# Eight places for the last Q, K, V rows, their summed stores on GpSimd's queue, and three small operations moved behind their neighbours

## The chip, the core and the metric

The kernel runs on one core of a Trainium2 chip. A core has a matrix engine (TensorE, PE in the rows), a vector engine (VectorE, DVE), a scalar engine (ScalarE, ACT), GpSimd (POOL) and a queue engine (SyncE, SP). Each engine works through its own list of instructions in order; engines wait for each other by semaphores. Three of them issue transfers (DMAs): SP, ACT and POOL, each by a queue of its own, and all transfers are served by the same 16 DMA engines. The metric is the device time of one launch in microseconds; lower is better.

## What is computed

The reference is one transformer block in float32 with attention and feed-forward side by side, for 2048 tokens of width 576:

```python
xn = _layernorm(x)                               # no learned scale
# attention: 32 heads of 18; token s sees s, s-2, ..., s-14
qkv = (xn @ wqkv).reshape(B, S, 3, H, Dh)
idx = pos[:, None] - 2 * arange(8)[None, :]
attn = softmax(where(idx >= 0, q . k[idx] * 18 ** -0.5, -1e9))
a = (attn @ v[idx]) @ wo
# feed-forward: 576 -> 4608 -> 576
h = xn @ w1 + b1
r = where(h > 0, h, 0)
out = x + a + (r * r) @ w2 + b2
```

## The kernel before

**Numbers in two parts.** The matrix engine takes a rounded float32 form. Each operand is kept as a rounded part ("hi", written by ACT as a copy) and the remainder ("lo", written by DVE as the operand minus hi). A product is three matmuls: hi x hi, hi x lo, lo x hi. So nearly every operand costs one ACT and one DVE instruction before PE may use it.

**Stages.** The tokens are four blocks of 512. The launch forms Q, K and V of blocks 0 and 1, runs their feed-forward pairs with block 0's second projection, then block 1's second projection; from about 547 us it forms Q, K and V of blocks 2 and 3 together (`phase_b0`, `quad_step`), then runs the feed-forward pairs of blocks 2 and 3 (`ffn_pair` with `s` = 1, pairs `p` = 0 to 17), and last block 3's second projection. The change lies where `quad_step` ends and the pairs begin, at about 612 to 685 us.

**`quad_step`.** The products of two token blocks with two weight groups are formed in seven products for eight (a Strassen scheme), in seven steps `s` for two chains `i`. Steps 4 to 7 each end one output row of 128 tokens by 432 numbers: ACT copies it from PSUM into a place of the tile `st` (line 1050); where a second term is to be added (steps 4 and 6), DVE adds it there (`tt`, line 108, form 128x432); then a DMA writes the place to the DRAM scratch `kvq` (line 1054). Rows without a sum are stored from ACT's queue, rows with a sum from SP's. `st` has four places, taken in turn (`rows_out % NJ`). A place is written again once the store before it has landed. 32 rows are stored; the last eight belong to the last of four half rounds, and its last two steps stand inside the first feed-forward pair as filler.

**`ffn_pair`.** For two token blocks and two 128-wide slices of the hidden layer it again forms seven products, T2, T3 and so on, in three PSUM banks `ba`, `bb`, `bc`. Two intermediates are copied out of `bb` by ACT: `u[:, 0]` (line 691, after T2) and `u[:, 1]` (line 723, after T3); PE may write the next product into `bb` only after that copy. DVE adds `bc` and `u[:, 1]` into `r1` (line 108, `r<-p,r`); PE may write the next product (B22) into `bc` only after that. Between the products stands the projection of the pair before (`work`, line 536, seven matmuls each).

**The small stacks.** From pair 2 on the 32 left-over input rows are packed into one extra matmul per product. Pair 1 prepares that: `stack_hi` (ACT, line 562) and `stack_lo` (DVE, forms 32x1024 and 32x512 `w1r<-w1r`) split the packed rows `LR["st"]`; `left_weight_hi` (ACT, line 595) and `left_weight_lo` (DVE, 64x896) split the weights. The unpacked rows come from DRAM by six loads `w1r<-xl` (line 552) on SP's queue, into a tile of the two-buffer pool `w1r`.

**Attention as side work.** `side(k)` does the next k steps of an attention generator on DVE: products `pr<-q,kv`, sums `lg<-pr`, then a maximum and a subtraction, then a step that begins with the exponential on ACT (line 396, `lg<-lg`) and goes on with a sum, a reciprocal and a product on DVE. `side(k, False)` stops ahead of the step with the exponential.

**What sets the order.** The program is written out by hand: each engine runs its instructions in the order in which the code emits them. DMAs raise counters that are taken in turn, eight for SP and ACT together and eight for POOL. A DMA that is to raise a counter first waits until the DMA eight places before it in the program, which raised the same counter, has landed.

Of the kernel before, what the change touches and what calls it, by code (L numbers as in the profile page):

```python
# [8 lines left out]
F32 = mybir.dt.float32  # L9
# [7 lines left out]
P = 128  # L17
# [4 lines left out]
NJ = TB // P  # L22
# [5 lines left out]
CG = HG * DH  # L28
QW = 3 * CG
# [10 lines left out]
T1, T3, B11, T2, B22, B21, LEFT, T4 = range(8)  # L40
# [5 lines left out]
def block_kernel(ctx: ExitStack, tc: tile.TileContext, x, xt, wqkv, wo, w1, b1, w2, b2, w1l, out):  # L46
    nc = tc.nc
    const = ctx.enter_context(tc.tile_pool(name="const", bufs=1))
    mt = ctx.enter_context(tc.tile_pool(name="mt", bufs=1))
    sb = ctx.enter_context(tc.tile_pool(name="sb", bufs=1))  # L50
# [56 lines left out]
    def tt(out, a, b, op):  # L107
        return nc.vector.tensor_tensor(out=out, in0=a, in1=b, op=op)  # L108
# [204 lines left out]
    qp, stage = {}, {}  # L313
# [107 lines left out]
    def side(k, exp=True):  # L421

        while k > 0:
            if current[0] is None:
                if not queue or queue[0][0] not in landed:
                    return k
                name, make = queue.pop(0)
                current[:] = [make(), None, name]
            if current[1] == "exp" and not exp:
                return k  # L430
            try:
                current[1] = next(current[0])
                k -= 1
            except StopIteration:
                current[0] = None
        return 0
# [38 lines left out]
    def w1_hi(n, k):  # L475
        w1s[n, k] = mt.tile([P, 2, 4, 2 * P], F32R, name="w1s", bufs=3)
        nc.scalar.activation(w1s[n, k][:, 0], raw1[n][:, 4 * k:4 * k + 4], AF.Copy)  # L477
# [33 lines left out]
    def w2_lo():  # L511
        i = los[0]
        los[0] += 1
        if i >= len(stream):
            return
        w = w2s[stream[i]]
        tt(w[:, DE:], raw2.pop(i)[:, :D], w[:, :D].bitcast(F32), ALU.subtract)
        load_w2(i + 3)
# [25 lines left out]
    ST, LW, LR = {}, {}, {}  # L544
# [16 lines left out]
    def stack_hi(to, v):  # L561
        nc.scalar.activation(to, v, AF.Copy)

    def stack_lo(to, v):
        rows = slice(L, 2 * L)
        tt(to[rows], v[rows], to[rows].bitcast(F32), ALU.subtract)
# [27 lines left out]
    def left_weight_hi(p):  # L594
        nc.scalar.activation(LW[p % 2], LR["w"], AF.Copy)

    def left_weight_lo(p):
        rows = slice(2 * L, P)
        tt(LW[p % 2][rows], LR["w"][rows], LW[p % 2][rows].bitcast(F32), ALU.subtract)
        load_left_weights(p + 1)  # L600
# [4 lines left out]
    def ffn_pair(s, p, work, first=False):  # L605
# [75 lines left out]
            stack_hi(LR["st"][:, 0:2], LR["a"][:, 0:2])  # L681
            stack_hi(ST[T4], LR["a"][:, 3])
        if not first:
            side(1 if p == 1 else 3 if s else 2 + p % 2, s == 1)
        work(0)
        product(bb, T2, ss(2))
        own_w2 = first and s == 1
# [10 lines left out]
        def splits():  # L698
            if not own_w2:
                w2_lo()  # L700
            if not last and not s:
                w1_hi(n + 1, 0)
            if ready:
                left_weight_hi(p + 1)
            if s and p == 1:
                stack_lo(LR["st"][:, 0:2], LR["a"][:, 0:2])
                stack_lo(ST[T4], LR["a"][:, 3])
                stack_hi(ST[T1], LR["s"][:, 0])
            if not own_w2:
                w2_hi()  # L710
            if not last and not s:
                w1_lo(n + 1, 0)
            if ready:
                left_weight_lo(p + 1)
            if not own_w2:
                w2_lo()

        if not first:
            splits()
# [3 lines left out]
        nc.scalar.activation(u[:, 1], bb, AF.Copy)  # L723
        r0, r1 = four(), four()
        tt(r1[:, 1], bc, u[:, 1], ALU.add)
        if first:
            splits()
        if not last and s:
# [298 lines left out]
    rows_out = [0]  # L1027

    def quad_step(k, s, j, i):
        b0, b1, gs = 2, 3, (2 * k, 2 * k + 1)  # L1030
        a, b, c, u = [bank(n)[:, :QW] if opened is None else opened for n, opened in
                      zip((*QKV_BANKS[i], i), quad_banks[i])]
        quad_banks[i] = [a, b, c, u]
        js = slice(j * P, (j + 1) * P)

        def product(to, name, v, start=False):
            mm = [(v(0, n), ws[name][0][:, n]) for n in range(2)]
            for n in range(2):
                mm += [(v(0, n), ws[name][1][:, n]), (v(1, n), ws[name][0][:, n])]
            for n, (l, r) in enumerate(mm):  # L1040
                nc.tensor.matmul(to, l[:, js], r, start=start and n == 0, stop=n == len(mm) - 1, skip_group_check=True)  # L1041

        def left(to, f, v):
            for n in range(2):
                nc.tensor.matmul(to, v[:, js], ws[LEFT, f][:, n], start=False, stop=n == 1, skip_group_check=True)  # L1045

        def row(n, f, x, y=None):
            st = stage[0][:, rows_out[0] % NJ]
            rows_out[0] += 1
            nc.scalar.activation(st, x, AF.Copy)  # L1050
            if y is not None:
                tt(st, y, st, ALU.add)
            to = kvq[gs[f]][:, PAD + n * TB:PAD + (n + 1) * TB].rearrange("i (p j) c -> p j i c", j=NJ)[:, j]
            (nc.sync if y is not None else nc.scalar).dma_start(to, st.rearrange("p (i c) -> p i c", c=CG))

        ss = lambda n: lambda h, q: SS[n][:, h, q]
        if s == 1:
            product(a, B11, lambda h, q: X[b0][:, h, q], start=True)
            nc.scalar.activation(b, a, AF.Copy)
        if s == 2:  # L1060
            product(c, T1, ss(1), start=True)
        if s == 3:
            product(b, T2, ss(2))
            nc.scalar.activation(u, b, AF.Copy)
        if s == 4:
            left(c, 1, x4[b1])
            product(b, T3, ss(3))
            row(b1, 1, b, c)
        if s == 5:
            product(a, B21, lambda h, q: X[b0][:, h, 2 + q])  # L1070
            left(a, 0, x4[b0])
            row(b0, 0, a)
        if s == 6:
            product(c, B22, lambda h, q: X[b1][:, h, q])
            left(c, 1, x4["d"])
            row(b0, 1, c, u)
        if s == 7:
            product(b, T4, lambda h, q: X[b1][:, h, 2 + q])
            left(b, 0, x4[b1])
            row(b1, 0, b)  # L1080
# [3 lines left out]
    def phase_b0():  # L1084
# [41 lines left out]
        def hook(k, half, s, i):  # L1126
            at = (k, half, s, i)
            if at == (0, 0, 1, 1):
                fourth_slot(0)
            if at == (0, 0, 2, 1):  # L1130
                load_half(1, 0)
                load_sides(1)
            if at == (0, 0, 5, 0):
                split_slot(B22, raw[0, 1][:, 1])
                load_half(1, 1)
            if half and not k:
                v, w, b21, b22 = raw[1, 0][:, 0], raw[1, 0][:, 1], raw[1, 1][:, 0], raw[1, 1][:, 1]
                if (s, i) == (1, 1):
                    slot(B11)
                    slot_hi(B11, v)  # L1140
                if (s, i) == (2, 0):
                    slot_lo(B11, v)
                if (s, i) == (2, 1):
                    tt(v, w, v, ALU.subtract)
                    slot(T1)
                    slot_hi(T1, v)
                if (s, i) == (3, 0):
                    tt(w, b22, w, ALU.subtract)
                if (s, i) == (3, 1):
                    slot_lo(T1, v)  # L1150
                if (s, i) == (5, 0):
                    tt(v, b22, v, ALU.subtract)
                    slot(T2)
                    slot_hi(T2, v)
                if (s, i) == (5, 1):
                    slot_lo(T2, v)
                    tt(v, b21, v, ALU.subtract)
                    slot(B21)
                    slot_hi(B21, b21)
                if (s, i) == (4, 1):  # L1160
                    slot(T3)
                    slot_hi(T3, w)
                    slot_lo(B21, b21)
                if (s, i) == (7, 0):
                    slot_lo(T3, w)
                if (s, i) == (7, 1):
                    fourth_slot(1)
                    split_side(1, 0)
                if (s, i) == (6, 1):
                    split_side(1, 1)  # L1170
                    split_slot(B22, b22)
                    kept_back[0] = 1
                    for g in (0, 1):
                        offer(2, g)
            if half and k:
                if (s, i) == (2, 1):
                    w1_again(NP, 0, nc.sync)
                if (s, i) == (5, 1):
                    complete(1)
                if (s, i) == (4, 1):  # L1180
                    w1_again(NP, 1, nc.sync)
            if kept_back[0] and not due(1):
                regroup(b, 0)
                fetch()
# [436 lines left out]
```

## Time and profile before

| | |
|---|---|
| median of 3 runs | 1107.96 us (1107.72 to 1108.0) |
| the profiled execution | 1107.93 us, its span 1106.2 us, 13892 instructions |
| PE, matmuls | 1096.8 us busy, 99% of the span |
| DVE | 912.0 us, 82% |
| ACT | 575.0 us, 52% |
| POOL | 115.4 us, 10% |
| DMA | 287.83 MB, mean 260 GB/s |

A row of a timeline has the start in us, the duration in us, the engine, the line, the operation with its tiles (out<-in), shapes and a count; in brackets stands how long the engine was idle before it and what ended that. Rows of equal instructions are merged, so the duration is that of the whole group. A row with "q" after the engine's name (SPq, ACTq) is the issue of a DMA. Line 108 is the helper of all DVE additions and subtractions, so those are told apart by their tiles.

### The profile page before, as it was taken

The page shows a single profiled execution, that of the slowest core. Times are in us where ns is not written, and L with a number is a line of the kernel's source. Part 1 is how long each engine was busy: PE and PEld are TensorE (multiplying, and loading weights), DVE is VectorE, ACT ScalarE, POOL GpSimd, SP SyncE. Part 2 cuts the span into 40 slices and gives each one's busy share as a digit, 9 for nine tenths or more (in the row PEclk, how much of TensorE's full clock was granted, in tenths as well). Part 3 has the DMA queues.
Part 4 walks back from the last instruction along what each step waited for, and adds up shares of the span by engine and source line. Part 5 has one row for each costly group of instructions (what it writes and reads, how often), then busy time and mean ns, then how long its engine had stood idle before and what let it go on. Part 6 is the DMA issues. An engine that isn't in the chain of part 4 may idle for free.

```text
span 1106.2 us, 13892 instructions
## 1 busy us (share of the span) xinstructions
PE 1096.8 (99%) x4950; PEld 925.2 (84%) x4950; DVE 912.0 (82%) x1223; ACT 575.0 (52%) x809; POOL 115.4 (10%) x219
## 2 busy tenths in 40 slices
PE   9999999999999999999999999999999999999998
PEld 7998888888888888888899887888888888888887
DVE  7696979897996979999979488978988789899654
ACT  5435666556566654455344355555555555533342
POOL 4000101020020100100010200202102021000100
PEclk9999999999999999999999999999999999999999
DMA  8956987889699686866755887768686785866752
GB/s 297 329 177 234 333 309 255 296 214 372 229 244 392 220 357 214 311 247 226 259 164 169 309 263 300 259 260 308 238 315 240 267 314 205 316 208 205 280 193 81
DMA packets 100279, 287.83 MB, mean 260 GB/s; under 512 B 13288, under 2 KB 41712, under 8 KB 85488
## 3 DMA queue, kind: packets, MB, share of 16 engines
q1 hardware_dynamic: 65280, 188.15, 49.1%
q0 software_dynamic: 10544, 52.14, 12.9%
q10 hardware_dynamic: 24384, 46.64, 12.6%
q8 instruction: 39, 0.64, 0.2%
q14 instruction: 32, 0.26, 0.1%
HBM read 205.14 MB, written 81.74 MB: 259 GB/s over the span
## 4 chain that ended last, share of the span: by engine, by line
PE 89%; DVE 5%; DMA 3%; ACT 1%; issue 1%; ACTq 0%; POOL 0%; DVEq 0%; POOLq 0%; SPq 0%
PE p L536 46%; PE p L629 31%; PE p L1041 5%; PE p L635 3%; DMA kvq<-st 2%; PE p L338 1%; PE p L1401 1%; PE p L1045 1%; DVE pr L108 1%; DMA kv<-kvq 1%; DVE lg L387 1%; DVE w1r L108 1%; DVE r L108 0%; PE p L1318 0%; DVE h L108 0%
## 5 line engine op out<-in xcount | busy, mean ns | idle before, releaser
L536 PE MATMUL p<-h,w2s 128*128 128x512 f32 x2066 | 491.4, 389 | 0.1
L536 PEld LDWEIGHTS p<-h,w2s 128*128 128x128 f32 x2066 | 387.5, 188 | 81.5 <-ACT h L642 0.6
L629 PE MATMUL p<-X,w1s 128*128 128x512 f32 x864 | 219.7, 389 | 1.2 <-DVE r L108 0.9
L629 PEld LDWEIGHTS p<-X,w1s 128*128 128x128 f32 x864 | 162.0, 188 | 35.6 <-DVE r L108 1.3
L509 ACT ACTIVATE w2s<-w2r 128x640 fp32r<-128x640 f32 x164 | 120.2, 735 | 116.1 <-PE p L536 87.6
L629 PE MATMUL p<-S,w1s 128*128 128x512 f32 x648 | 164.8, 390 | 1.5 <-ACT r L691 1.5
L108 DVE TENSOR_TENSOR w2s<-w2r,w2s 128x576 fp32r<-128x576 f32 x164 | 123.4, 753 | 40.6 <-ACT w2s L509 39.8
L629 PEld LDWEIGHTS p<-S,w1s 128*128 128x128 f32 x648 | 121.4, 188 | 27.4 <-ACT r L691 2.3
L415 POOL DMA_DIRECT2D o<-q x128 | 69.2, 605 | 584.8 <-DVE q L108 582.8
L638 ACT ACTIVATE r<-r,b1t 128x512 f32<-128x512 f32 x72 | 52.0, 723 | 126.9 <-DVE r L108 125.2
L387 DVE TENSOR_REDUCE lg<-pr 128x64 f32<-128x1152 f32 x64 | 86.5, 1352 | 1.5
L108 DVE TENSOR_TENSOR pr<-lg,kv 128x1152 f32<-128x1152 f32 x64 | 86.7, 1354 | 1.3
L108 DVE TENSOR_TENSOR pr<-q,kv 128x1152 f32<-128x1152 f32 x64 | 86.6, 1353 | 0.8
L108 DVE TENSOR_TENSOR pr<-pr 128x576 f32<-128x576 f32 (+1 forms) x128 | 77.5, 605 | 3.2
L646 ACT ACTIVATE r<-r 128x1024 f32<-128x1024 f32 x72 | 76.1, 1057 | 1.2
L108 DVE TENSOR_TENSOR h<-r,h 128x1024 fp32r<-128x1024 f32 (+3 forms) x46 | 51.8, 1136 | 27.0 <-ACT r L646 18.8
L108 DVE TENSOR_TENSOR r<-p,r 128x512 f32<-128x512 f32 (+1 forms) x77 | 52.9, 688 | 20.3 <-PE p L629 9.8
L108 DVE TENSOR_TENSOR w1s<-w1r,w1s 128x1024 fp32r<-128x1024 f32 (+1 forms) x42 | 50.3, 1198 | 16.5 <-ACT w1s L477 16.4
L691 ACT ACTIVATE r<-p 128x512 f32<-128x512 f32 x36 | 21.5, 597 | 70.9 <-PE p L629 70.5
L638 ACT ACTIVATE r<-p,b1t 128x512 f32<-128x512 f32 x72 | 48.3, 672 | 0.0
L108 DVE TENSOR_TENSOR h<-h 128x1024 fp32r<-128x1024 f32 x36 | 43.9, 1220 | 4.8 <-ACT h L938 4.6
L536 PE MATMUL p<-w1s,w2s 128*128 128x512 f32 x195 | 44.7, 389 | 0.0
(193 smaller groups left out, 1174.2 us busy)
## 6 DMA issues: line engine op xcount, KB each, us to landing
w2r<-in_w SPq DMA_DIRECT2D x144, 320.0 KB, 3.4
kv<-kvq POOLq DMA_DIRECT2D x29, 1296.0 KB, 9.4
w<-w1s SPq DMA_DIRECT2D x36, 1024.0 KB, 8.4
w1s<-w ACTq DMA_DIRECT2D x34, 1024.0 KB, 7.3
h<-r SPq DMA_DIRECT2D x36, 512.0 KB, 6.3
h<-h SPq DMA_DIRECT2D x36, 512.0 KB, 4.2
w1r<-in_w SPq DMA_DIRECT2D x18, 640.0 KB, 7.7
kvq<-st ACTq DMA_DIRECT2D x48, 216.0 KB, 3.2
```

Source lines behind the costliest of these rows:

```text
L108: return nc.vector.tensor_tensor(out=out, in0=a, in1=b, op=op)
L338: nc.tensor.matmul(p[:, :QW], l, r, start=k == 0, stop=k == len(mm) - 1)
L387: nc.vector.tensor_reduce(out=lg[:, j * HG:(j + 1) * HG].rearrange("p a w -> p w a"), in_=pr.rearrange("p w (a d) -> p w a d", d=DH), axis ...
L415: nc.gpsimd.dma_start(rows[:, i], q[i * L:(i + 1) * L, :, a:z])
L509: nc.scalar.activation(w2s[stream[i]][:, :DE], raw2[i], AF.Copy)
L536: nc.tensor.matmul(yp[b][c], v, a, start=c not in yb[b], stop=c in last and c not in [o[0] for o in ops[i + 1:]], skip_group_check=True)
L629: nc.tensor.matmul(to, l, r, start=start and i == 0, stop=i == len(mm) - 1, skip_group_check=True)
L635: nc.tensor.matmul(to, weight(LEFT, k, f), v, start=False, stop=k == 1, skip_group_check=True)
L638: nc.scalar.activation(to, a, AF.Relu, bias=b1t[:, f:f + 1])
L646: nc.scalar.activation(r, r, AF.Square)
L691: nc.scalar.activation(u[:, 0], bb, AF.Copy)
L1041: nc.tensor.matmul(to, l[:, js], r, start=start and n == 0, stop=n == len(mm) - 1, skip_group_check=True)
```

## The change

Four edits. (1) At step (3, 0) of the last half round a second tile of four places is opened, from the pool `w1r`. The places then alternate between the two tiles: rows 25 to 28 go to the new ones, rows 29 to 32 to the old ones. (2) From then on the rows with a sum are stored from GpSimd's queue, not from SP's. (3) In pair 1 the two remainders `stack_lo(LR["st"]...)` and `stack_lo(ST[T4]...)` stand behind the addition that reads `bc`, not in `splits()` between two w2 remainders. (4) In pair 2 the first `side` call stops ahead of the exponential, which so comes with the next `side` call. The order of PE's instructions is the same in both kernels.

```diff
         if not first:
-            side(1 if p == 1 else 3 if s else 2 + p % 2, s == 1)
+            side(1 if p == 1 else 3 if s else 2 + p % 2, s == 1 and p != 2)
...
             if s and p == 1:
-                stack_lo(LR["st"][:, 0:2], LR["a"][:, 0:2])
-                stack_lo(ST[T4], LR["a"][:, 3])
                 stack_hi(ST[T1], LR["s"][:, 0])
...
         r0, r1 = four(), four()
         tt(r1[:, 1], bc, u[:, 1], ALU.add)
+        if s and p == 1:
+            stack_lo(LR["st"][:, 0:2], LR["a"][:, 0:2])
+            stack_lo(ST[T4], LR["a"][:, 3])
...
         def row(n, f, x, y=None):
-            st = stage[0][:, rows_out[0] % NJ]
+            places = stage[(rows_out[0] // NJ + 1) % len(stage)]
+            st = places[:, rows_out[0] % NJ]
...
-            (nc.sync if y is not None else nc.scalar).dma_start(to, st.rearrange("p (i c) -> p i c", c=CG))
+            (nc.scalar if y is None else nc.sync if len(stage) < 2 else nc.gpsimd).dma_start(to, st.rearrange("p (i c) -> p i c", c=CG))
...
             if half and k:
+                if (s, i) == (3, 0):
+                    stage[1] = sb.tile([P, NJ, QW], F32, name="w1r", bufs=2)
```

**ACT at the last eight rows.** ACT's list from the copy of row 25 on, first as it stood. `kvq_98` is the scratch for the rows without a sum; "waits" names the counters that the row waits for (DMAHW3: a transfer of SP or ACT; PE, DVE, Activation: that engine).

```order
L1050 ACTIVATE st<-p_4688 128x432 [waits DMAHW3_49,PE_49]
L1054 DMA kvq_98<-st 128x3x144 [waits Activation_49]
L1050 ACTIVATE st<-p_4689 128x432 [waits DMAHW6_49,PE_49]
L1050 ACTIVATE st<-p_4699 128x432 [waits DMAHW5_49,PE_49]
L1054 DMA kvq_98<-st 128x3x144 [waits Activation_49]
L1050 ACTIVATE st<-p_4700 128x432 [waits DMAHW7_49,PE_49]
L1050 ACTIVATE st<-p_4689 128x432 [waits DMAHW1_49,PE_49]
L1054 DMA kvq_98<-st 128x3x144 [waits Activation_49]
L1050 ACTIVATE st<-p_4690 128x432 [waits DMAHW2_49,DVE_49,PE_49]
L663 ACTIVATE p_5310<-p_5309 128x512 [waits PE_49]
L487 DMA w1s<-w_113 128x2048 [waits DMAHW0_49]
L1050 ACTIVATE st<-p_4700 128x432 [waits DMAHW3_49,PE_49]
```

The same stretch of ACT's list with the change:

```order
L1052 ACTIVATE w1r<-p_4688 128x432 [waits PE_49]
L1056 DMA kvq_98<-w1r 128x3x144 [waits Activation_49]
L1052 ACTIVATE w1r<-p_4689 128x432 [waits PE_49]
L1052 ACTIVATE w1r<-p_4699 128x432 [waits PE_49]
L1056 DMA kvq_98<-w1r 128x3x144 [waits DMAHW2_49,Activation_49]
L1052 ACTIVATE w1r<-p_4700 128x432 [waits PE_49]
L1052 ACTIVATE st<-p_4689 128x432 [waits DMAHW3_49,PE_49]
L1056 DMA kvq_98<-st 128x3x144 [waits DMAHW4_49,Activation_49]
L1052 ACTIVATE st<-p_4690 128x432 [waits DMAHW6_49,PE_49]
L663 ACTIVATE p_5311<-p_5310 128x512 [waits PE_49]
L487 DMA w1s<-w_113 128x2048 [waits DMAHW5_49]
L1052 ACTIVATE st<-p_4700 128x432 [waits PE_49]
```

The copies of row 31 (the last row shown) and of row 32 no longer wait for a store of this half round (before, row 31 waited for DMAHW3, raised by the store of row 27, the second ACT store shown); the second ACT store now waits for the counter DMAHW2.

**SP in the same place.** SP's list before, from the load of the first half of block 2's weights (`w_111`, its second half is `w_112`):

```order
L487 DMA w1s<-w_111 128x2048 [waits DMAHW0_49,PE_49,Activation_49]
L1054 DMA kvq_99<-st 128x3x144 [waits DMAHW2_49,DVE_49]
L1054 DMA kvq_99<-st 128x3x144 [waits DMAHW4_49,DVE_49]
L487 DMA w1s<-w_112 128x2048 [waits DMAHW5_49,PE_49,Activation_49]
L1054 DMA kvq_99<-st 128x3x144 [waits DMAHW7_49,DVE_49]
L1054 DMA kvq_99<-st 128x3x144 [waits DMAHW2_49,DVE_49]
L552 DMA w1r<-xl_147 32x2x512 [waits DMAHW4_49,Activation_49]
L552 DMA w1r<-xl_148 32x2x512 [waits DMAHW5_49]
```

And with the change:

```order
L487 DMA w1s<-w_111 128x2048 [waits DMAHW0_49,PE_49,Activation_49]
L487 DMA w1s<-w_112 128x2048 [waits DMAHW1_49,PE_49,Activation_49]
L552 DMA w1r<-xl_147 32x2x512 [waits DMAHW2_49,Activation_49]
L552 DMA w1r<-xl_148 32x2x512 [waits DMAHW3_49]
L552 DMA w1r<-xl_147 32x2x512 [waits DMAHW5_49]
L552 DMA w1r<-xl_148 32x2x512 [waits DMAHW6_49]
L552 DMA w1r<-xl_147 32x2x512 [waits DMAHW7_49]
L552 DMA w1r<-xl_148 32x2x512 [waits DMAHW0_49]
L586 DMA mb<-in_w1l 128x512 [waits DMAHW1_49]
L1222 DMA h<-y_185 128x2048 [waits DMAHW3_49,PE_49]
```

The four stores that waited for DVE are gone from SP's list, so the second half of the weights, the six `xl` loads, a weight load and the megabyte `h<-y` stand directly behind the first half. On POOL the first of the four stores stands between a load `kv<-kvq` and the two loads `kv<-o`, the other three behind those.

**DVE in pair 1.** Before, from the first w2 remainder of `splits()` on:

```order
L108 TENSOR_TENSOR w2s<-w2r,w2s 128x576
L108 TENSOR_TENSOR w1r<-w1r 32x1024
L108 TENSOR_TENSOR w1r<-w1r 32x512
L108 TENSOR_TENSOR w2s<-w2r,w2s 128x576
L108 TENSOR_TENSOR r_5631<-p_5558,r_5601 128x512
L108 TENSOR_TENSOR w1r<-kv,w1r 32x512
```

With the change:

```order
L108 TENSOR_TENSOR w2s<-w2r,w2s 128x576 x2
L108 TENSOR_TENSOR r_5630<-p_5559,r_5602 128x512
L108 TENSOR_TENSOR w1r<-w1r 32x1024
L108 TENSOR_TENSOR w1r<-w1r 32x512
L108 TENSOR_TENSOR w1r<-kv,w1r 32x512
```

The addition that frees `bc` (`r<-p,r`) stands ahead of the two remainders instead of behind them.

**DVE in pair 2.** Before, from the maximum of the attention on; the exponential on ACT stands between the second and the third row:

```order
L393 TENSOR_REDUCE mx<-lg 128x32
L108 TENSOR_TENSOR lg<-lg,mx 128x256
L397 TENSOR_REDUCE sm<-lg 128x32
L398 RECIPROCAL sm<-sm 128x32
L108 TENSOR_TENSOR lg<-lg,sm 128x256
L108 TENSOR_TENSOR pr<-lg,kv 128x1152
L108 TENSOR_TENSOR w2s<-w2r,w2s 128x576
L108 TENSOR_TENSOR w1r<-mb,w1r 64x896
L108 TENSOR_TENSOR w2s<-w2r,w2s 128x576
L108 TENSOR_TENSOR r_5783<-p_5698,r_5753 128x512
```

With the change:

```order
L393 TENSOR_REDUCE mx<-lg 128x32
L108 TENSOR_TENSOR lg<-lg,mx 128x256
L108 TENSOR_TENSOR w2s<-w2r,w2s 128x576
L108 TENSOR_TENSOR w1r<-mb,w1r 64x896
L108 TENSOR_TENSOR w2s<-w2r,w2s 128x576
L108 TENSOR_TENSOR r_5778<-p_5699,r_5748 128x512
L397 TENSOR_REDUCE sm<-lg 128x32
L398 RECIPROCAL sm<-sm 128x32
L108 TENSOR_TENSOR lg<-lg,sm 128x256
L108 TENSOR_TENSOR pr<-lg,kv 128x1152
```

Four rows of the attention moved behind the addition. On ACT the exponential moved from ahead of a w2 copy (line 509) and the `u[:, 0]` copy (line 691) to behind the two ReLUs that follow them (line 638). The attention is two steps later from there on, until pair 4, where both lists agree again.

## Prediction

> **What bounds the kernel.** I read the page's busy times first, then the waits of PE, then PE's timeline where those waits lie, and last the other engines and the DMA issues in the 70 us around it.
>
> ```profile
> PE 1096.8 (99%) x4950; PEld 925.2 (84%) x4950; DVE 912.0 (82%) x1223; ACT 575.0 (52%) x809; POOL 115.4 (10%) x219
> PE p L1318 <- DVE lg L1311: 2.1, 1, 2.1
> PE p L629 <- ACT r L691: 1.5, 2, 0.8
> PE p L629 <- DVE r L108: 0.9, 1, 0.9
> PE p L629 <- DVE w1s L108: 0.3, 1, 0.3
> ```
>
> PE is busy for 1096.8 us of a span of 1106.2. Nothing that leaves PE's work alone can win more than the 9.4 us between. The list of PE's waits (us in total, times, longest) says where a part of it lies: 2.1 us at the start, and three single waits on line 629, two for the copy of line 691 and one for a DVE addition (the fourth, 0.3 us, waits for a weight). All three lie between 621 and 690 us:
>
> ```profile
> 630.21 1.65 PE L629 MATMUL p<-S,w1s 128*128 128x512 f32 x6 [0.85 <-ACT r L691]
> 666.02 1.65 PE L629 MATMUL p<-X,w1s 128*128 128x512 f32 x6 [0.93 <-DVE r L108]
> 669.78 1.75 PE L536 MATMUL p<-h,w2s 128*128 128x512 f32 x7
> 671.36 1.52 PE L629 MATMUL p<-X,w1s 128*128 128x512 f32 x6
> 680.16 1.66 PE L629 MATMUL p<-S,w1s 128*128 128x512 f32 x6 [0.70 <-ACT r L691]
> ```
>
> A stop costs more than the idle time in brackets. Undisturbed groups overlap: seven matmuls last 1.75 us in the row at 669.78, yet the next group begins 1.58 us later, so a stop loses 0.17 us of overlap; and six matmuls last 1.65 after a stop against 1.52 without one, 0.13 more. Each stop therefore costs its idle time + 0.30: 1.15, 1.23 and 1.00 us, 3.38 us together. The PE list itself is unchanged, so the change is worth whatever part of this 3.38 goes, less what it puts in its place.
>
> **First stop: the places (new places, and stores on GpSimd).** ACT's rows, with the landing of one DMA (KB, us from issue to landing):
>
> ```profile
> 617.82 0.37 ACTq L1054 DMA_DIRECT2D kvq<-st  x1
> kvq<-st ACTq DMA_DIRECT2D x1, 216.0 KB, 10.7
> 628.59 0.53 ACT L1050 ACTIVATE st<-p 128x432 f32<-128x432 f32 x1 [4.46 <-DMA kvq<-st]
> 629.56 0.60 ACT L691 ACTIVATE r<-p 128x512 f32<-128x512 f32 x1 [0.44 <-PE p L1045]
> 626.28 1.52 PE L629 MATMUL p<-S,w1s 128*128 128x512 f32 x6
> ```
>
> The store of row 27, issued at 617.82, took 10.7 us. Row 31 needs its place and sits ahead of the copy of line 691 on ACT, so that copy began at 629.56 although its input (T2, the PE row at 626.28) was done at 627.8. With eight places row 31's copy waits only for PE; it would run at about 626.3, its store issue ends by 627.3, and the copy of line 691 runs from 627.8 to 628.4. PE wants it at 629.36 (630.21 less 0.85): 1.0 us to spare. Gain 1.15. The copies and additions themselves are the same in number; they write another tile.
>
> The stores move the queues. SP's and POOL's rows, and landings:
>
> ```profile
> 607.66 4.86 PE L1041 MATMUL p<-w1s,S 128*128 128x432 f32 x24
> 616.89 3.49 SPq L1054 DMA_DIRECT2D kvq<-st  x2
> 620.49 0.46 SPq L487 DMA_DIRECT2D w1s<-w  x1
> w1s<-w SPq DMA_DIRECT2D x1, 1024.0 KB, 5.0
> w1s<-w SPq DMA_DIRECT2D x1, 1024.0 KB, 11.1
> 631.70 4.90 SPq L552 DMA_DIRECT2D w1r<-xl  x6
> w1r<-xl SPq DMA_DIRECT2D x6, 128.0 KB, 8.4
> 617.48 0.76 POOL L845 DMA_DIRECT2D kv<-o  x1
> 619.61 0.55 POOL L845 DMA_DIRECT2D kv<-o  x1 [1.37 <-issue]
> kv<-o POOLq DMA_DIRECT2D x1, 384.0 KB, 8.0
> ```
>
> The second weight half (issue at 620.49, landing 11.1 us, 631.6) stood behind two stores that waited for DVE. Its buffer is free when T2's last matmul of `quad_step` ends, 612.5 (PE row at 607.66). So it will go at about 612.5, eight us sooner, and the six `xl` loads from about 613 instead of 631.70. That is a gain for a load that was only just in time, and costs SP nothing: nothing else on SP is late. On POOL four stores are added. None of its issues is for 384 runs of 576 bytes, so their price is bounded: 0.55 us as the `kv<-o` row, or three times 0.76 = 2.3 us if it goes by the number of runs (128 there). I take 1.6 (three times 0.55); four of them are 6.4 us on an engine that is 10% busy. Only the first stands ahead of the loads `kv<-o`, and delays them by 0.6 to 2.3 us. The later landed at 627.6 (619.61 + 8.0), and is wanted here:
>
> ```profile
> 634.11 1.30 DVE L869 STREAM_TRANSPOSE r<-kv 128x512 f32<-128x512 f32 x2
> 637.73 12.86 PE L536 MATMUL p<-h,w2s 128*128 128x512 f32 x56
> ```
>
> PE uses the result at 637.73, and one transpose (0.65) and one ACT copy lie between: landing as late as 635.2 (with PE 1.15 sooner) would do. Over 5 us of cover; cost nothing, and if the cover goes, one us per us.
>
> **Second stop: the remainders.** DVE's rows and two of ACT's:
>
> ```profile
> 661.86 0.75 DVE L108 TENSOR_TENSOR w2s<-w2r,w2s 128x576 fp32r<-128x576 f32 x1
> 662.64 1.82 DVE L108 TENSOR_TENSOR w1r<-w1r 32x1024 fp32r<-32x1024 f32 x2
> 664.48 0.76 DVE L108 TENSOR_TENSOR w2s<-w2r,w2s 128x576 fp32r<-128x576 f32 x1
> 665.27 0.69 DVE L108 TENSOR_TENSOR r<-p,r 128x512 f32<-128x512 f32 x1
> 668.17 1.09 DVE L108 TENSOR_TENSOR w1r<-mb,w1r 64x896 fp32r<-64x896 f32 x1 [1.50 <-ACT w1r L595]
> 660.42 0.74 ACT L509 ACTIVATE w2s<-w2r 128x640 fp32r<-128x640 f32 x1 [0.97 <-ACT w1r L562]
> 661.73 0.60 ACT L723 ACTIVATE r<-p 128x512 f32<-128x512 f32 x1 [0.57 <-PE p L629]
> ```
>
> The two remainders (1.82) move behind `r<-p,r`. The w2 remainder at 664.48 can start at 662.64, as its ACT half was done at 661.16; the addition then runs at 663.4 to 664.1, its ACT input done at 662.33. PE wants it at 665.09: 1.0 us to spare, where 0.88 was missing. Gain 1.23. The 1.82 us now fall before the 64x896 remainder, ahead of which DVE stood idle for 1.50; that remainder ends no later than before, and PE first uses it in pair 2, behind the group at 671.36.
>
> **Third stop: the exponential.**
>
> ```profile
> 676.12 1.52 PE L629 MATMUL p<-S,w1s 128*128 128x512 f32 x6
> 678.12 0.42 DVE L108 TENSOR_TENSOR lg<-lg,mx 128x256 f32<-128x256 f32 x1
> 676.22 0.62 ACT L562 ACTIVATE x4d<-kv 128x512 fp32r<-128x512 f32 x1
> 678.58 0.42 ACT L396 ACTIVATE lg<-lg 128x256 f32<-128x256 f32 x1 [1.74 <-DVE lg L108]
> 678.90 0.72 ACT L509 ACTIVATE w2s<-w2r 128x640 fp32r<-128x640 f32 x1
> 679.53 0.58 ACT L691 ACTIVATE r<-p 128x512 f32<-128x512 f32 x1
> ```
>
> ACT ended its last stack copy at 676.84 and then stood 1.74 us for the attention's subtraction, with the w2 copy and the copy of line 691 queued behind. Without the exponential there, the w2 copy runs at 676.9 to 677.6, and line 691's copy follows T2, which ends at 677.9 (the group at 676.12 and one more matmul): 677.9 to 678.5. PE wants it at 679.46; 1.0 us to spare. Gain 1.00. What is late next is the attention: two steps, made up by pair 4. Ahead of the pair's first addition DVE has four attention rows fewer, ahead of the second one four rows where four stood. I cost that at nothing: no step is added, and the list of waits has no stop of PE by DVE in the later pairs that is longer than 0.3 us.
>
> **Sum.** 1107.93 (profiled execution; the median is 1107.96) - 1.15 - 1.23 - 1.00 = 1104.55; I say 1104.5. The stops go one after another, but each is tied to PE's own progress before it, so one gain doesn't eat the next.
>
> **Rivals.** *ACT stops for a counter.* With the change ACT's second store, ready at 617.82, waits for DMAHW2, which the first `xl` load raises, and that load stands behind two megabytes of weights on SP's queue. Three copies wait behind it. The last of them (row 30, about 2.5 us after the wait ends) must be done before PE's next group in that bank:
>
> ```profile
> 623.35 1.52 PE L629 MATMUL p<-S,w1s 128*128 128x512 f32 x6
> ```
>
> So the wait is free up to 620.85 and costs PE the excess + 0.30 beyond. The load goes at about 613.2. If it lands in the 8.4 us of the `xl` row, 621.6, the stop is 1.05 and the time 1105.6. If it takes the 11.1 of the congested weight half, 624.3, the stop is 3.75 and the time 1108.3, slower than before; from a landing of 10.7 us on it makes the kernel slower, from 13.0 us on by over 0.2% (1110.2). For it: a 216 KB store took 10.7 us four us later. Against it: those long landings began with the loads POOL issued from 617 on; before them a whole megabyte landed in 5.0, at 615.2. A second one that began only then and took as long would land at 620.2, still ahead of 620.85 with the 128 KB behind it; the two overlap, so I take 618.5, an ACT wait of 0.7 us, hidden. [...] By the trace's 11.1 the rival would hold; the trace has no load in that place, so this rival keeps 0.14: 0.04 for a small stop below 1105.7, 0.06 up to 1110.2, 0.04 beyond.
>
> *GpSimd's loads come late.* The `kv<-o` loads land after 635.2, each us costing one. It needs 7.6 us on top of the 627.6; if they took the 11.1 us of the weight half behind 2.3 us of issue, they would land at 633, and the time is unchanged. At 637 the time is 1106.3. [...] 0.03.
>
> *The DVE addition is still late.* The w2 copy on ACT at 660.42 followed 0.97 us of idleness that no ACT row explains, so a w2 load ended it; if that load lands over 1.0 us later among the moved transfers, part of the second stop comes back, up to 1.23: 1105.7. 0.08, 0.05 of it with most of the gain kept.
>
> *Nothing is won:* another wait behind each of the three takes its place, 1107.9. 0.04.
>
> **Chances.** The forecast has 0.71; the four rivals 0.14, 0.03, 0.08, 0.04. A measurement tells about 0.2% here, 2.2 us, so faster means below 1105.7: the forecast, 0.04 of the first rival and 0.05 of the third, 0.80. Same 0.16 (0.06, 0.03, 0.03 and 0.04), slower the first rival's 0.04. The range is 1104.0 (the weight half's small waits gone too) to 1106.6, which leaves out the long landings, late loads and the last case; the forecast's own is 1104.0 to 1105.2.
>
> **What would show it.** PE's list of waits keeps the 2.1 at the start and loses all three of line 629. ACT's row of the exponential stands behind ReLUs; the second weight half is issued near 612.5; the first `xl` load has landed by 619; ACT's third and fourth copies to `st` wait for PE, not for a DMA; GpSimd's four stores show their issue time. I am wrong if PE stops anew at 623 (counter), at 636 (GpSimd), or in pairs 3 and 4 (attention).

## The result

The changed kernel takes 1105.03 us (median of 22 runs, 1104.32 to 1108.53), the kernel before in the same rounds 1107.66 us (22 runs, 1106.77 to 1110.01). The ratio is 0.9981, with a 95% interval of 0.9974 to 0.9988: a gain of 2.1 us, between 1.3 and 2.9 (the medians differ by 2.6). The forecast was 3.4.

The profiled execution of the changed kernel took 1104.87 us, its span is 1103.2 (before: 1107.93 and 1106.2). Its busy times hardly differ; only GpSimd has four instructions and 3.5 us more:

```profile
PE 1096.6 (99%) x4950; PEld 925.8 (84%) x4950; DVE 911.7 (83%) x1223; ACT 575.5 (52%) x809; POOL 118.9 (11%) x223
```

PE's list of waits (us in total, times, longest) answers the first question of the prediction. The three stops of line 629 are gone, and one of 0.2 us is new (the list has one more row, 0.2 us on line 536 at about 113 us, far from the change):

```profile
PE p L1322 <- DVE lg L1315: 2.1, 1, 2.1
PE p L629 <- ACT st L1052: 0.2, 1, 0.2
```

In PE's timeline the groups at 629.97, 664.42 and 677.57 are those that stood behind the old stops; none has idle time ahead of it, and each lasts 1.52. The new stop is at 623.95:

```profile
621.98 1.55 PE L629 MATMUL p<-X,w1s 128*128 128x512 f32 x6
623.95 1.65 PE L629 MATMUL p<-S,w1s 128*128 128x512 f32 x6 [0.20 <-ACT st L1052]
629.97 1.52 PE L629 MATMUL p<-S,w1s 128*128 128x512 f32 x6
664.42 1.52 PE L629 MATMUL p<-X,w1s 128*128 128x512 f32 x6
677.57 1.52 PE L629 MATMUL p<-S,w1s 128*128 128x512 f32 x6
679.15 1.52 PE L629 MATMUL p<-X,w1s 128*128 128x512 f32 x6
```

The first and the last of these rows give a measure that the rest of the text uses, called the **stretch** here: from the start of the first feed-forward group to the start of the group behind the third old stop. It takes in all that the change touches and leaves out what differs from one execution to the next elsewhere. Now it is 679.15 - 621.98 = 57.17 us. Before, the same two rows are these, 60.12 us apart:

```profile
621.76 1.52 PE L629 MATMUL p<-X,w1s 128*128 128x512 f32 x6
681.88 1.52 PE L629 MATMUL p<-X,w1s 128*128 128x512 f32 x6
```

So the stretch gained 2.95 us where the prediction had 3.38. ACT's rows show where the difference sits:

```profile
614.91 0.37 ACTq L1056 DMA_DIRECT2D kvq<-w1r  x1
619.98 0.37 ACTq L1056 DMA_DIRECT2D kvq<-w1r  x1
620.39 0.53 ACT L1052 ACTIVATE w1r<-p 128x432 f32<-128x432 f32 x1 [2.38 <-DMA w1r<-xl]
622.90 0.37 ACTq L1056 DMA_DIRECT2D kvq<-st  x1
623.37 0.53 ACT L1052 ACTIVATE st<-p 128x432 f32<-128x432 f32 x1 [2.02 <-DMA kvq<-w1r]
627.21 0.53 ACT L1052 ACTIVATE st<-p 128x432 f32<-128x432 f32 x1 [2.82 <-PE p L1046]
628.60 0.60 ACT L691 ACTIVATE r<-p 128x512 f32<-128x512 f32 x1 [0.86 <-PE p L629]
```

ACT's second store was issued at 619.98, held by the counter of the first `xl` load: the wait that the first rival named, inside its limit of 620.85. Its third store was then held until 622.90, by a second counter, DMAHW4. That one was last raised by ACT's own first store, issued at 614.91, 8.0 us earlier. The copy queued behind the third store, that of row 30, ran at 623.37, and PE waited for it. The copy of row 31 (627.21), which a store held up in the kernel before, and the copy of line 691 (628.60), late there, now wait for PE alone.

What the moved queues did, in SP's and POOL's rows and in three landings (KB, us from issue to landing):

```profile
612.81 0.33 SPq L487 DMA_DIRECT2D w1s<-w  x1
613.23 3.11 SPq L552 DMA_DIRECT2D w1r<-xl  x6
```

```profile
619.33 0.56 POOL L360 DMA_DIRECT2D kv<-kvq  x1 [1.95 <-DMA o<-q]
620.75 0.79 POOL L1056 DMA_DIRECT2D kvq<-w1r  x1 [0.86 <-issue]
622.82 0.54 POOL L846 DMA_DIRECT2D kv<-o  x1 [0.71 <-DMA o<-q]
```

```profile
w1s<-w SPq DMA_DIRECT2D x1, 1024.0 KB, 6.5
w1r<-xl SPq DMA_DIRECT2D x2, 128.0 KB, 6.7
kv<-o POOLq DMA_DIRECT2D x1, 384.0 KB, 10.1
```

The second weight half went at 612.81 and landed at 619.3, the first `xl` load at 619.9. A store of 384 runs costs GpSimd 0.79 us. Nevertheless the later `kv<-o` load was issued 3.2 us later than before (622.82 against 619.61), since POOL had waited for its own small stores `o<-q`, and landed at 632.9. GpSimd's new stores are not the reason: in the last kernel of the experiments, which has none of them there, this load goes at 622.72.

DVE's and ACT's rows at the second and third old stop:

```profile
662.79 0.69 DVE L108 TENSOR_TENSOR r<-p,r 128x512 f32<-128x512 f32 x1
663.52 1.82 DVE L108 TENSOR_TENSOR w1r<-w1r 32x1024 fp32r<-32x1024 f32 x2
```

```profile
674.98 0.73 ACT L509 ACTIVATE w2s<-w2r 128x640 fp32r<-128x640 f32 x1
676.18 0.60 ACT L691 ACTIVATE r<-p 128x512 f32<-128x512 f32 x1 [0.47 <-PE p L629]
681.91 0.40 ACT L396 ACTIVATE lg<-lg 128x256 f32<-128x256 f32 x1
```

The addition `r<-p,r` now runs ahead of the remainders (1.82) and ends at 663.5, 0.9 us ahead of PE's group at 664.42. In pair 2 the w2 copy runs at once, the copy of line 691 waits for PE alone and ends 0.8 us ahead of PE's group at 677.57, and the exponential follows at 681.91.

### The profile page after: what moved, and what is told of

Read it like the earlier page. It is cut to its first block, busy times and chain, and to the rows that moved or that the text cites. A ratio compares the mean times of both kernels' runs of the same rounds, so it can differ in the third digit from the quotient of the medians.

```text
span 1103.2 us, 13891 instructions
## 1 busy us (share of the span) xinstructions
PE 1096.6 (99%) x4950; PEld 925.8 (84%) x4950; DVE 911.7 (83%) x1223; ACT 575.5 (52%) x809; POOL 118.9 (11%) x223
## 4 chain that ended last, share of the span: by engine, by line
PE 96%; DVE 2%; DMA 1%; issue 1%; ACT 0%; ACTq 0%; POOL 0%; DVEq 0%; POOLq 0%
PE p L536 45%; PE p L629 33%; PE p L338 7%; PE p L1042 5%; PE p L635 3%; PE p L1405 1%; PE p L1046 1%; DMA kvq<-w1r 1%; DVE pr L108 0%; DVE w2s L108 0%; PE p L1322 0%; DVE h L108 0%; DVE w1s L108 0%; PE p L1367 0%; DVE r L108 0%
```

## The experiments

Two theories were tried. Theory A: each old stop is worth its idle time + 0.30, and what is missing is ACT's wait for young transfer counters. A counter is called young here when the transfer that raised it last was issued only a few us before, so that it may not have landed. Rival B: the shortfall comes from elsewhere. A gain outside the stretch, or a stretch that changes without a stop, would speak for B. Unless said otherwise, the diffs are against the changed kernel. Medians are of 11 runs and the ratios are to the kernel before, which took 1107.54 (33 runs) beside four of the kernels (no places, places alone, ACT without stores, `xl` later) and 1107.95 (28 runs) beside the other four.

**One part at a time.** The remainders and the exponential without places (the stores with sums then stay on SP):

```diff
-                if (s, i) == (3, 0):
-                    stage[1] = sb.tile([P, NJ, QW], F32, name="w1r", bufs=2)
```

> The kernel before with the moved remainders and the moved exponential alone; the last eight rows have their four places and SP's queue as before. Theory A (each stop is worth its idle time + 0.30, and what the whole change lost against its forecast is ACT's wait for transfer counters): the second and third stop go, 1.23 + 1.00, the first stays: 2.2 us under the kernel before, about 1105.4. PE's waits keep the one of 0.85 at 630. Rival B (the loss comes from the moved remainders or the later attention, for instance in later pairs): less than 1.5 us won here.

Measured: 1105.34 us, ratio 0.9982 (0.9973 to 0.9991). The places and the stores alone, with the other two edits undone:

```diff
-            side(1 if p == 1 else 3 if s else 2 + p % 2, s == 1 and p != 2)
+            side(1 if p == 1 else 3 if s else 2 + p % 2, s == 1)
...
             if s and p == 1:
+                stack_lo(LR["st"][:, 0:2], LR["a"][:, 0:2])
+                stack_lo(ST[T4], LR["a"][:, 3])
                 stack_hi(ST[T1], LR["s"][:, 0])
...
-        if s and p == 1:
-            stack_lo(LR["st"][:, 0:2], LR["a"][:, 0:2])
-            stack_lo(ST[T4], LR["a"][:, 3])
```

> The kernel before with the eight places and the stores on GpSimd's queue alone. Theory A: the first stop goes (1.15), a new one at 623 comes (0.2 idle in the profile, 0.4 to 0.5 with its restart; more in executions where the transfers take longer): 0.3 to 0.8 us under the kernel before, about 1107.1. Rival B: the full 1.15 is won here, about 1106.5.

Measured: 1107.05 us, ratio 0.9996 (0.9987 to 1.0004). PE's waits of line 629 in the two, first without places, then with nothing but these:

```profile
PE p L629 <- ACT r L691: 0.7, 1, 0.7
```

```profile
PE p L629 <- DVE r L108: 0.9, 1, 0.9
PE p L629 <- ACT st L1051: 0.7, 1, 0.7
PE p L629 <- ACT r L691: 0.6, 1, 0.6
```

Without places one old stop stays, the first. With them alone the other two stay, and in place of the first there is the new one near 623, 0.7 us long in this execution. Nearly the whole gain of the change is that of the remainders and the exponential; the places and the queue alone can't be told from no gain (the interval holds 1). Each of the two small edits alone, on the kernel before:

```diff
-                stack_lo(LR["st"][:, 0:2], LR["a"][:, 0:2])
-                stack_lo(ST[T4], LR["a"][:, 3])
...
         tt(r1[:, 1], bc, u[:, 1], ALU.add)
+        if s and p == 1:
+            stack_lo(LR["st"][:, 0:2], LR["a"][:, 0:2])
+            stack_lo(ST[T4], LR["a"][:, 3])
```

> The kernel before with the two remainders moved, and nothing else. By the sum of the prediction PE loses the stop behind the DVE addition alone, 0.93 + 0.30: 1107.5 - 1.2 = 1106.3 (1106.0 to 1106.7); the two stops of line 629 behind ACT's copy of line 691 stay, 0.85 and 0.70. Rival: the stops hang together (what one wins the next loses), and the time is 1107.5 with the later stop longer by what the earlier won.

Measured: 1106.56 us, ratio 0.9988 (0.9979 to 0.9997); stretch 58.86, 1.26 shorter than before.

```diff
-            side(1 if p == 1 else 3 if s else 2 + p % 2, s == 1)
+            side(1 if p == 1 else 3 if s else 2 + p % 2, s == 1 and p != 2)
```

> The kernel before with the exponential kept back in the second half of pair 2, and nothing else. By the sum of the prediction PE loses the third stop alone, 0.70 + 0.30: 1107.5 - 1.0 = 1106.5 (1106.2 to 1106.9); the first stop behind ACT's copy of line 691 (0.85) and the one behind the DVE addition (0.93) stay. Rival: the attention, two steps late, costs PE a wait in pairs 3 to 5, and the time is 1107.0 or more.

Measured: 1106.47 us, ratio 0.9991 (0.9982 to 1.0, just reaching 1); stretch 58.96, 1.16 shorter. The waits of the two, remainders first:

```profile
PE p L629 <- ACT r L691: 1.1, 2, 0.7
PE p L635 <- DMA w1s<-w: 0.3, 1, 0.3
```

```profile
PE p L629 <- DVE r L108: 0.9, 1, 0.9
PE p L629 <- ACT r L691: 0.4, 1, 0.4
```

Both edits take just their own stop away, and no wait for the late attention appears. The first stop is shorter in both executions (0.45 and 0.43), and in both the first use of the weight half (line 635) then comes about 0.3 late, as if the longer stop of the kernel before had covered that load.

**The places with the old queue.** The stores with sums stay on SP, so the second weight half stands behind two of them again:

```diff
-            (nc.scalar if y is None else nc.sync if len(stage) < 2 else nc.gpsimd).dma_start(to, st.rearrange("p (i c) -> p i c", c=CG))
+            (nc.sync if y is not None else nc.scalar).dma_start(to, st.rearrange("p (i c) -> p i c", c=CG))
```

> The changed kernel, but the four stores with sums stay on SP, in their old order: the second weight half stands behind two of them again, issued at about 620.5 as in the kernel before. ACT waits for no young counter, so it makes no stop at 623. Theory A: the weight half lands at about 631.6 as before, and PE, 1.15 us earlier, wants it at 630.55; PE stops at line 635 for it for about 1.0 + 0.3 us, the first stop's gain is gone, and the time is 1107.5 - 2.2 = 1105.3 (1104.8 to 1105.8). If the weight half lands by 630.5 after all (nothing else is congested differently), the time is 1104.1 and the earlier weight half was worth nothing. Rival B: 1105.0 without a stop of PE at line 635.

Measured: 1105.9 us, ratio 0.9981 (0.9972 to 0.999). SP's issue of the weight half, its landing, and PE's row:

```profile
619.90 0.46 SPq L487 DMA_DIRECT2D w1s<-w  x1
```

```profile
w1s<-w SPq DMA_DIRECT2D x1, 1024.0 KB, 11.0
```

```profile
630.96 0.73 PE L635 MATMUL p<-x,w1s 128*128 128x512 f32 x2 [0.78 <-DMA w1s<-w]
```

The load lands at 630.9 and PE stops for it, 0.78 where 1.0 was expected. With the places PE comes too early for this load: the earlier weight half is not an extra, the first stop can't be won without it.

**ACT without stores.** Of the last eight stores SP takes the four that were ACT's, GpSimd keeps its four, and the weight half is asked for ahead of them:

```diff
-            (nc.scalar if y is None else nc.sync if len(stage) < 2 else nc.gpsimd).dma_start(to, st.rearrange("p (i c) -> p i c", c=CG))
+            (nc.gpsimd if y is not None and len(stage) > 1 else nc.sync if y is not None or len(stage) > 1 else nc.scalar).dma_start(to, st.rearrange("p (i c) -> p i c", c=CG))
...
-                if (s, i) == (4, 1):
+                if (s, i) == (3, 1):
                     w1_again(NP, 1, nc.sync)
```

> The changed kernel, but ACT issues none of the last eight stores: SP stores the four without a sum, GpSimd the four with one, and the second half of block 2's weights is asked for one step sooner, so that it stays ahead of those stores on SP. ACT's copies then wait for PE alone. Theory A: the new stop at 623 goes, none of the old comes back: about 3.4 us under the kernel before, 1104.2, and 0.4 us or more under the changed kernel's 1105.0, with a narrower spread. Rival B (the missing part isn't ACT's waits): same time as the changed kernel, within 0.2 us.

Measured: 1105.6 us, ratio 0.9979 (0.997 to 0.9988); the expected 1104.2 was missed. The stop near 623 is gone, but ACT still issues weight loads, and one of these met a young counter. ACT's rows and PE's:

```profile
635.24 0.34 ACTq L487 DMA_DIRECT2D w1s<-w  x1
635.62 0.72 ACT L638 ACTIVATE r<-r,b1t 128x512 f32<-128x512 f32 x1 [4.62 <-DMA w1r<-xl]
```

```profile
637.49 13.00 PE L536 MATMUL p<-h,w2s 128*128 128x512 f32 x56 [1.23 <-ACT h L871]
```

The load at 635.24 waited for DMAHW6, raised by SP's store of row 31, which was issued at 626.67 and took 8.5 us to land. (The bracket names an `xl` load, but the first of these was issued at 627.08 and took 9.3: it had not landed.) The copies behind it came late, and PE stopped for 1.23. So the cause is the same in kind, at another place and by another transfer.

**The `xl` loads later**, behind the megabyte `h<-y` on SP's queue:

```diff
-                load_left_rows()
                 LR["w"] = sb.tile([P, 7, P], F32, name="mb")
...
                 nc.sync.dma_start(xr[b][0], yscr)
+                load_left_rows()
```

> The changed kernel with the six loads of the packed rows (xl) behind the megabyte h<-y on SP's queue. By the order of the program ACT's store of row 29 then waits for the counter of h<-y, a load that is issued near 617. Theory A: ACT stands there until that megabyte has landed, near 626, and PE's stop at 623 grows to 3 us or more: 1108 or above, slower than the kernel before. Rival B: ACT's counters are harmless, the time stays at the changed kernel's 1105.

Measured: 1106.05 us, ratio 0.9993 (0.9984 to 1.0002), in two groups: six runs from 1105.31 to 1106.05, five from 1106.97 to 1109.41. The median misses the 1108 that was expected; four runs of the upper group, the profiled one (1108.24) among them, do not. By the order of the program the counter of ACT's third store was last raised by the megabyte `h<-y`, issued at 615.85 in this run. ACT's third store and PE:

```profile
624.73 0.37 ACTq L1056 DMA_DIRECT2D kvq<-st  x1
```

```profile
620.74 1.54 PE L629 MATMUL p<-X,w1s 128*128 128x512 f32 x6
625.78 2.52 PE L629 MATMUL p<-S,w1s 128*128 128x512 f32 x6 [3.27 <-ACT st L1052]
682.54 1.52 PE L629 MATMUL p<-X,w1s 128*128 128x512 f32 x6
```

**Without young counters.** The stores with sums on SP again, but the second weight half ahead of those of the last four rows. ACT's stores then wait only for transfers of eight or more us before:

```diff
-            (nc.scalar if y is None else nc.sync if len(stage) < 2 else nc.gpsimd).dma_start(to, st.rearrange("p (i c) -> p i c", c=CG))
+            (nc.sync if y is not None else nc.scalar).dma_start(to, st.rearrange("p (i c) -> p i c", c=CG))
...
-                if (s, i) == (4, 1):
+                if (s, i) == (3, 1):
                     w1_again(NP, 1, nc.sync)
```

> The changed kernel, but the four stores with sums stay on SP, and the second weight half is asked for at step (3, 1), ahead of those of the last four. ACT's four stores then wait for counters of transfers issued eight or more us earlier only (the third for a store of SP of about 609, the fourth for the weight half of about 612), and the xl loads go at about 631 as before. Theory A (each of the three old stops is worth its idle time + 0.30, and what is missing from 3.38 us in the changed kernel is ACT's wait for transfer counters): PE has no stop of line 629, and the time is 1107.5 - 3.4 = 1104.1, at most 1104.6, with no runs above 1106. Rival B (the shortfall lies elsewhere: in the places themselves, or a part of the gain is taken back behind the stage): 1105.0 as the changed kernel, although no stop of line 629 is left.

Measured: 1104.35 us (6 runs, 1102.92 to 1105.09), ratio 0.9968 (0.9955 to 0.998). PE's timeline at both ends of the stretch, and ACT's third store, issued 0.81 us before the stretch begins (in the changed kernel 0.92 after it):

```profile
621.76 1.52 PE L629 MATMUL p<-X,w1s 128*128 128x512 f32 x6
678.38 1.52 PE L629 MATMUL p<-X,w1s 128*128 128x512 f32 x6
```

```profile
620.95 0.37 ACTq L1056 DMA_DIRECT2D kvq<-st  x1
```

The stretch is 56.62 us, 3.50 shorter than before: the prediction's 3.38 and 0.12 more. The same kernel again, beside the changed one on one chip (before there: 1107.71, 17 runs):

> The kernel with the stores with sums on SP and the second weight half ahead of them, a second time, beside the changed kernel on the same chip. Theory A: 1104.2 again (1103.9 to 1104.6), no stop of PE on line 629 between 621 and 690, no run above 1106. Rival B: no better than the changed kernel beside it.

> The changed kernel itself, beside the former. Theory A: 0.5 to 1.0 above it in the median, with single runs above 1106, and in the profile a stop of PE on line 629 near 623.9 whose size is what ACT's third store waits for its counter, beyond the cover of its copies. Rival B: the same time as the former, within 0.3, or the difference without a stop near 623.9.

Measured: 1104.17 us (5 runs, 1103.61 to 1105.53, ratio 0.9964, 0.9951 to 0.9977) against 1105.61 (12 runs, 1104.64 to 1112.22, ratio 0.9991, 0.9977 to 1.0005). The former is the best of all kernels here; the changed kernel's interval holds 1 in these rounds. Its profiled run, the 1105.53, has the stretch of 56.62 once more; it lost 1.2 us by a wait for a weight at 94 us, far from the change. The changed kernel in its second profile, ACT and PE:

```profile
623.20 0.37 ACTq L1056 DMA_DIRECT2D kvq<-st  x1
```

```profile
620.79 1.52 PE L629 MATMUL p<-X,w1s 128*128 128x512 f32 x6
624.25 1.67 PE L629 MATMUL p<-S,w1s 128*128 128x512 f32 x6 [1.71 <-ACT st L1052]
679.46 1.52 PE L629 MATMUL p<-X,w1s 128*128 128x512 f32 x6
```

The stop is 1.71 here, and the stretch 58.67: the 1.15 us of the first stop are lost again, and 0.86 more (1.71 + 0.30 - 1.15). Two more profiles of the changed kernel were to test the relation between ACT's store, the stop and the stretch:

> The changed kernel, one profile more, to see how its time varies. Theory A: PE's stop on line 629 near 623 is the issue of ACT's third store, counted from the start of the stage's first group of line 629, less 0.71 us (0.92 gave 0.20 and 2.41 gave 1.71 in the two profiles so far), and the stage from there to the start of the group behind the third old stop lasts 56.62 us + that stop + 0.30. Rival: the stage's length varies without that stop.

> As the other look: stop near 623 = (issue of ACT's third store - start of the stage's first group of line 629) - 0.71 us, stage 56.62 us + stop + 0.30; in a run above 1106.9 the stop is 2 us or more. Rival: a long run whose stop near 623 is under 1 us.

Measured: 1104.92 and 1104.45 us. The first has its third store at 622.99, 1.06 after the stretch begins (621.93), so a stop of 0.35 was expected and 0.33 found:

```profile
624.04 1.66 PE L629 MATMUL p<-S,w1s 128*128 128x512 f32 x6 [0.33 <-ACT st L1052]
```

Its stretch is 57.32 (expected 57.25). In the second the store went at 622.43, 0.78 after the beginning at 621.65; the expected stop, 0.07, is too short to be listed, and the stretch is 57.02 (expected 56.99). The same relation gives 0.72 for the places alone (found: 0.71) and 3.28 for `xl` later (3.27). Neither run was above 1106.9, so that part stays untested.

All stretches side by side. "Stops" are PE's listed waits inside it; the sum is 56.62, the stretch of the last row, + each stop + 0.30 for each:

| kernel | stops | sum | stretch |
|---|---|---|---|
| before | 0.85, 0.93, 0.70 | 60.00 | 60.12 |
| remainders alone | 0.45, 0.25, 0.65 | 58.87 | 58.86 |
| exponential alone | 0.43, 0.92 | 58.57 | 58.96 |
| no places | 0.65 | 57.57 | 57.94 |
| places alone | 0.71, 0.93, 0.65 | 59.81 | 59.86 |
| places, old queue | 0.78 | 57.70 | 57.75 |
| ACT without stores | 1.23, 0.22 | 58.67 | 58.71 |
| `xl` later | 3.27 | 60.19 | 61.80 |
| changed kernel, two profiles | 0.20; 1.71 | 57.12; 58.63 | 57.17; 58.67 |
| no young counters, two profiles | none | 56.62 | 56.62; 56.62 |

Two rows miss by 0.37 and 0.39: there PE's first group of line 635 begins about 0.34 late, where it takes up the weight half, too little for the list of waits. One misses by 1.61, of which more below. The rest agree within 0.12. That is theory A. As to B: outside the stretch the profiled spans vary from 1044.6 to 1047.2 us, by 1.0 in the best kernel alone, so single profiles don't exclude some tenths there. The runs speak against it: for the six kernels of the table other than the kernel before, the changed one, `xl` later and ACT without stores, the gain by the ratio agrees with that of the stretch within 0.5 us.

## Why the prediction was right, and where it was off

- **Sum and sign.** The median, 1105.03, lies in the forecast's own range (1104.0 to 1105.2), but the gain is about two thirds of the 3.38 by the ratio. That the median still lies in the narrow range is partly luck: the kernel before took 1107.66 in these rounds, 0.27 less than the 1107.93 of the sum. The three stops hold as a mechanism: stop plus 0.30 gave eight of the eleven stretches with a listed stop within 0.12, and 3.50 us are there to be had.
- **Second and third stop (1.23 and 1.00).** As worked out: 1.26 and 1.16 alone, and nothing late behind them. No PE wait for the attention is listed in the pairs of any profile. One reading of the third rival does not hold: the 0.97 us of ACT's idleness ahead of the w2 copy at 660.42 was put down to a w2 load, but the row with the change, where the transfers had moved, has the same 0.97 to the digit.
- **First stop (1.15): the mis-sized term.** What the prediction said of the places came true: ACT's third and fourth copies to `st` wait for PE (627.21 for row 31), and the copy of line 691 ran from 628.60 to 629.20, 0.8 us ahead of PE's group at 629.97. The step that failed is what the change puts in the place of the stop, which was priced at nothing. The prediction priced one counter, DMAHW2 on ACT's second store, and took row 30's copy to be done about 2.5 us after that wait ends. It was done 3.9 us after (619.98 to 623.90), since the third store stands between, with a wait of its own for DMAHW4. That wait has no price in the prediction, though it stands in ACT's list that was quoted with the change.

  So PE did stop anew at 623, the prediction's own sign of being wrong, if only for 0.20 us in the first profile. Against the 56.62 of the last kernel the four profiles of the changed kernel lost 0.55, 2.05, 0.70 and, without a listed stop, 0.40 us of the stretch. The counter's origin is ACT's own first store, which held the third one until 8.0 and 9.5 us after its issue in the first two profiles, where the megabytes and the `xl` loads were ahead of it; the same store landed 2.5 us after its issue (614.69) in the kernel before.
- **The counter rival.** The first `xl` load landed at 619.9, not 618.5, still inside 620.85: no stop by itself, as the forecast had it. The second of the two megabytes ahead of it landed at 619.3, 6.5 us after its issue.
- **GpSimd.** A store costs 0.74 to 0.79 us, near the lower bound of 0.55 and not the 1.6 taken. The cover of `kv<-o` was called "over 5 us". It landed at 632.9, and DVE's transpose that reads it began at 634.23: 1.3 us are left. The bound given (633) held, but the term that ate the cover was another: POOL's own `o<-q` stores, 2.1 to 2.2 us (median) from issue to landing before, 5.8 to 6.2 with the second weight half and the `xl` loads moved to 612.81 and after.
- **The weight half.** That it was only just in time was right, and it decides: with the places but without its move the stop comes back at line 635.

The times of the changed kernel have a tail (3 of the first 22 runs and 5 of the 12 beside the best kernel lie above 1106.9, up to 1112.22) that the best kernel lacks (none of 11 above 1105.53). The wait for the counter, whose length varied by 1.5 us between two profiles, would explain it, but no profile caught such a run: that is argued, not shown. One number speaks for it: the mean granted clock of PE is 0.997 or 0.998 in six of these eight runs, and in four runs of the kernel with the later `xl` loads, whose profile shows a long stop and a halved clock (last section). In all other runs whose clock is on record it is 0.999 or 1.000.

## What to carry to other kernels

With this program's eight counters in turn a DMA issue waited for the landing of the eighth transfer before it: ACT's third store until 622.90, 8.0 us after the issue of the store that had raised its counter. ACT also copies, and what stood behind that issue waited as well (row 30's copy until 623.37, and PE 0.20 us for it). So after any move of transfers list for each issue on a busy engine which transfer raised its counter before, when that one was issued, and what lay ahead of it in the queues (the counter of that store held ACT until 8.0 and 9.5 us after its issue with the megabytes and the `xl` loads ahead of it; in the kernel before it landed in 2.5). Where loads are brought forward, see that the transfers whose counters a busy engine takes up again were issued long before: here the order "weights early, small loads late" gave the whole gain, "everything early" about two thirds of it.

## What was not expected of the hardware

In the run with the stop of 3.27 us the stretch is 1.61 longer than the stop explains. The windows of that run show where it goes (the window and its length, busy us and count of PE, PEld, DVE, ACT, POOL, then the granted clock, the DMA share and GB/s):

```profile
625.60:627.00 1.40, 1.22 (x4) 1.01 (x5) 0.61 (x1) 0.61 (x2) 0.34 (x1) 0.74 0.97 348
627.00:628.00 1.00, 1.00 (x4) 0.81 (x3) 0.00 (x0) 0.00 (x0) 0.42 (x1) 0.50 1.00 350
628.00:629.00 1.00, 1.00 (x4) 0.86 (x3) 0.00 (x0) 0.00 (x0) 0.00 (x0) 0.50 1.04 353
629.00:630.00 1.00, 1.00 (x5) 0.94 (x4) 0.00 (x0) 0.00 (x0) 0.00 (x0) 0.65 1.08 369
630.00:631.00 1.00, 1.00 (x6) 0.89 (x6) 0.00 (x0) 0.41 (x1) 0.00 (x0) 1.00 1.03 355
```

The stop ended at 625.78. PE's granted clock is 0.74 on average from 625.6 to 627, 0.50 from 627 to 629, 0.65 in the next us and 1.00 again from 630 to 631. What is missing to the full clock adds up to 0.36 + 0.50 + 0.50 + 0.35 = 1.71 us, an estimate from these windows, against the 1.61. In the second profile of the changed kernel, with its stop of 1.71 us, the clock was 1.00 in every window from 622 to 628. So this stop of 3.27 us cost 1.61 us more than "idle + 0.30", half as much again as the stop itself. What lowers the clock was not shown: there is one profile with each of these two stops.
